# Loading q and k by head pairs in long runs: one window-attention and feed-forward kernel on one core

**Chip, cores, metric.** One Trainium2 chip, one core. The metric is the device time of one execution in microseconds (us). Runs of one set of comparisons share a chip; a run over 1.5% above the fastest of its kernel is slow, and comparisons use fast runs.

## The reference

```python
# q, k, v: (8 batches, 8 heads, 576 rows, 64), fp32; w_in 512x2048, w_out 2048x512
scores = q @ k.T / 8;  keep |i - j| <= 32;  attn = softmax(scores)
x = (attn @ v) as 4608 tokens x 512
h = x @ w_in;  g = h if h > 0 else exp(h) - 1
out = g @ w_out                                  # fp32
```

## The kernel before

The program is one loop of 144 steps. A step does the first layer of 256 hidden columns for 256 tokens (eight matmuls, an exponential on ScalarE, two VectorE operations) and, two steps later, the second layer (four matmuls). Attention is done in 36 pairs of 64-row blocks, placed between the steps. Four routes feed it, and these are what the change touches: q and k from DRAM, turned so that the head dimension lies on partitions; v, and a copy of it shifted by 64 partitions; and x, the attention's result, turned for the first layer.

```python
SJ = 6; SP_ = S // SJ                     # 96 partitions, 6 rows on each
def load_qk(b, which, part):              # part: whole batch or half
    z, nj = part
    ...
    nc.sync.dma_start(
        out=t[:, z * n:(z + 1) * n].rearrange("p (h x) -> p h x", h=H),
        in_=(q, k)[which][b, :, z * SP_ * nj:(z + 1) * SP_ * nj, :]
        .rearrange("h (p j) d -> p h (j d)", j=nj))

def rotate_v(b, m0=0, m1=VS - 1):         # the shifted copy of v
    e, o = V_e[b % 3], V_o[b % 3]
    nc.sync.dma_start(out=o[0:64, m0:m1], in_=e[64:128, m0:m1])
    nc.sync.dma_start(out=o[64:128, m0:m1], in_=e[0:64, m0 + 1:m1 + 1])

def transpose_rows(b, which):             # bf16 rows in DRAM -> qT or kT
    nc.sync.dma_start_transpose(
        out=keys_or_queries(b, which), in_=in_dram.pop((b, which)))

def x_dma(i):                             # pair i's x -> xT, also on SyncE
    x_st = st.pop(i)[3]
    nc.sync.dma_start_transpose(
        out=xT_of(i), in_=x_st.rearrange("p h d -> p (h d)"))

# ... (cut) the schedule: k0 is the step at which a batch's first pair begins
for b in range(2, B):
    k0 = begin[first_pair(b)]
    if b >= 3:
        kk = max(k0 - 26 if b < 5 else k0 - 36, 18)
        at(kk, "mid", load_qk, b, 0, WHOLE)
        at(kk + 1, "mid", load_qk, b, 1, WHOLE)
        for m in range(VS):
            at(kk + 2 + m // 3, "mid", load_v, b, m)
    if b < 5:   ...   # casts on POOL, transposes on TensorE
    else:       ...   # casts on ACT, rows to DRAM, transpose_rows
```

Batches 0 to 4 are turned by TensorE (casts for batches 2 to 4 on POOL, which is GpSimd), batches 5 to 7 by a DMA transpose of bf16 rows that were written back to DRAM. SyncE issues, in program order, the loads of q and k, the shifted copies, both kinds of DMA transpose and the outputs.

Names in the profile: PE is TensorE and PEld its weight loads, DVE is VectorE, ACT ScalarE, POOL GpSimd, SPq SyncE's queue. `f` is the tile in which q or k lands, `qkb` its bf16 cast, `Ve` is v and `Vo` its shifted copy, `in_dram` the rows written back, `x_st` and `xT` are x before and after its transpose. The granted clock is the share of TensorE's full clock that the chip allowed.

The softmax here doesn't subtract the row's maximum and nothing guards it: scores larger than these inputs give would overflow.

Of the kernel before, what the change touches and what calls it, by code (L numbers as in the profile page):

```python
# [9 lines left out]
FP32 = mybir.dt.float32  # L10
# [11 lines left out]
def kernel(  # L22
# [22 lines left out]
    SJ = 6  # L45
    SP_ = S // SJ
# [39 lines left out]
    def ps_tile(shape, dt, tag, name):  # L86
        return pools[tag].tile(shape, dt, tag=tag, name=name)
# [19 lines left out]
    def load_qk(b, which, part):  # L107
        z, nj = part
        if (b, which) not in qk_f:
            qk_f[b, which] = lpool.tile([SP_, H * SJ * D], FP32,  # L110
                                        tag=f"f{which}", name=f"f{which}")
        t = qk_f[b, which]
        n = H * nj * D
        nc.sync.dma_start(
            out=t[:, z * n:(z + 1) * n].rearrange("p (h x) -> p h x", h=H),
            in_=(q, k)[which][b, :, z * SP_ * nj:(z + 1) * SP_ * nj, :]
            .rearrange("h (p j) d -> p h (j d)", j=nj))
# [9 lines left out]
    def rotate_v(b, m0=0, m1=VS - 1):  # L127
        e, o = V_e[b % 3], V_o[b % 3]
        nc.sync.dma_start(out=o[0:64, m0:m1], in_=e[64:128, m0:m1])
        nc.sync.dma_start(out=o[64:128, m0:m1], in_=e[0:64, m0 + 1:m1 + 1])  # L130
# [41 lines left out]
    for m in (1, 2, 0, 3, 4):  # L172
        load_v(0, m)
    rotate_v(0, 0, 2)
    rotate_v(0, 2, VS - 1)
# [39 lines left out]
    def cast_qk(b, which, part, hps, eng):  # L215
        z, nj = part
        hp0, nh = hps[0], 2 * len(hps)
        n = H * nj * D
        s_ = qk_f[b, which][:, z * n + 2 * hp0 * nj * D:
                            z * n + (2 * hp0 + nh) * nj * D]  # L220
        s_ = _bap(s_, [s_.ap[0], [nj * D, nh], [D, nj], [1, D]])
        t = lpool.tile([SP_, nj, nh * D], BF16, tag=f"b{which}", name="qkb",
                       bufs=4)
        qk_b[b, which, z, hp0] = t
        copy_on(eng, _bap(t, [t.ap[0], [D, nh], [nh * D, nj], [1, D]]), s_)

    def keys_or_queries(b, which):
        if which == 0:
            return qT[b % 2]
        return kT[b % 2][:, KPAD:KPAD + HP * S].rearrange(  # L230
            "p (g s) -> p g s", g=HP)


    rows, in_dram = {}, {}

    def cast_rows(b, which, hp):
        if hp == 0:
            rows[b, which] = lpool.tile([SP_, SJ, H * D], BF16,
                                        tag=f"r{which}", name="rows", bufs=1)
        n = SJ * D  # L240
        s_ = qk_f[b, which][:, 2 * hp * n:(2 * hp + 2) * n]
        d_ = rows[b, which][:, :, 2 * hp * D:(2 * hp + 2) * D]
        nc.scalar.copy(  # L243
            _bap(d_, [d_.ap[0], [D, 2], [H * D, SJ], [1, D]]),
            _bap(s_, [s_.ap[0], [n, 2], [D, SJ], [1, D]]))

    def write_rows(b, which):
        t = dpool.tile([S, H * D], BF16, tag=f"d{which}", name="in_dram")
        in_dram[b, which] = t
        nc.scalar.dma_start(  # L250
            out=t.rearrange("(p j) c -> p j c", j=SJ), in_=rows.pop((b, which)))
# [5 lines left out]
    def transpose_qk(b, which, part, hps, evac, tag="t0"):  # L257
        z, nj = part
        src = qk_b.pop((b, which, z, hps[0]))
        nh = len(hps)  # L260
        W = 512 if nh > 1 else 1024
        pt = ps_tile([128, nh, W], BF16, tag, "ptx")
        for g in range(nh):
            for j in range(nj):
                nc.tensor.transpose(  # L265
                    pt[:, g, j * SP_:(j + 1) * SP_],
                    src[:, j, g * 128:(g + 1) * 128], ident[0:SP_, 0:SP_])
        n = SP_ * nj
        d = keys_or_queries(b, which)[:, hps[0]:hps[0] + nh, z * n:(z + 1) * n]
        pitch = d.ap[1][0] if nh > 1 else n  # L270
        copy_on(evac,
                _bap(d, [d.ap[0], [pitch, nh], [nj, SP_], [1, nj]]),
                _bap(pt, [pt.ap[0], [W, nh], [1, SP_], [SP_, nj]]))

# [70 lines left out]
    def x_evac(i):  # L345
        nc.vector.tensor_copy(xT_of(i), st.pop(i))  # L346
# [14 lines left out]
    def front_qk(part, tags):  # L361
        for g in range(2):
            hps = (2 * g, 2 * g + 1)
            cast_qk(0, 0, part, hps, nc.vector)
            cast_qk(0, 1, part, hps, nc.scalar)
            transpose_qk(0, 0, part, hps, nc.scalar, tags[g])
            transpose_qk(0, 1, part, hps, nc.vector, tags[2 + g])

    front_qk(HALF_A, ("h0", "h1", "y0", "y1"))
# [4 lines left out]
    front_qk(HALF_B, ("h0", "h1", "y0", "y1"))  # L374
    for fn in (pv, normalize, x_transpose, x_evac):
        for i in (0, 1):
            fn(i)
# [9 lines left out]
    rotate_v(1, 0, 2)  # L387
# [5 lines left out]
    rotate_v(1, 2, VS - 1)  # L393
# [25 lines left out]

    for i, tag in ((2, "s"), (3, "u")):  # L420
        at(0, "mid", scores, i, tag)
        at(1, "dve", mask, i)
        at(1, "mid", pv, i)
        at(2, "dve", normalize, i)
        at(2, "mid", x_transpose, i)
        at(3, "dve", x_evac, i)
    at(4, "dve", swap_pools)

    allh = tuple(range(HP))
    for part, kq in ((HALF_A, 8), (HALF_B, 16)):  # L430
        for which in range(2):
            at(kq - 1, "mid", cast_qk, 1, which, part, allh,
               (nc.scalar, nc.vector)[which])
            at(kq + which, "mid", transpose_qk, 1, which, part, allh,
               nc.scalar, "s")
    pair_at(4, 10)
    pair_at(5, 13)
# [5 lines left out]
    for i in range(8, NPAIR):  # L443
        kk = begin[i] = max(HALF * (i - 2) - 6, begin[i - 1] + 3)
        at(kk, "mid", scores, i)
        at(kk + 1, "dve", mask, i)
        at(kk + 1, "end", pv, i)
        at(kk + 2, "dve", normalize, i)
        at(kk + 2, "end", x_dma, i)
    for b in range(2, B):  # L450
        k0 = begin[first_pair(b)]
        if b >= 3:
            kk = max(k0 - 26 if b < 5 else k0 - 36, 18)
# [4 lines left out]
        if b < 5:  # L458
            for n in range(2 * HP):
                which, hp = n // HP, n % HP  # L460
                kk = k0 - (8 if b == 2 else 10) + n
                at(kk - 2 - b // 3, "mid", cast_qk, b, which, WHOLE, (hp,),
                   nc.gpsimd)
                at(kk, "mid", transpose_qk, b, which, WHOLE, (hp,), nc.scalar)
        else:
            for which in range(2):
                c0 = k0 - 27 + 8 * which
                for hp in range(HP):
                    at(c0 + (0, 1, 4, 5)[hp], "end", cast_rows, b, which, hp)
                at(c0 + 6, "mid", write_rows, b, which)  # L470
                at(c0 + 9, "mid", transpose_rows, b, which)
        at(k0 - HALF, "mid", rotate_v, b)
# [97 lines left out]
```

## Time and profile before

| | before |
|---|---|
| time, median (lowest to highest) | 337.28 us (336.18 to 338.95), 4 runs |
| profiled execution | span 340.9 us, granted clock 0.987 |
| first step, from the timeline | exponential at 28.2 us |
| last step | exponential at 333.2 us |

The prediction below shows the lines on which the reading of the kernel before rests: TensorE is busy nearly throughout, and the DMA engines for the first 150 us. Needed beside them are the landing times in the last part of its page (KB each, median us from issue to landing):

```profile
f<-in_q_dram SPq DMA_DIRECT2D x6, 1152.0 KB, 12.7
f<-in_k_dram SPq DMA_DIRECT2D x6, 1152.0 KB, 15.9
...
Ve<-in_v_dram POOLq DMA_DIRECT2D x24, 128.0 KB, 13.2
```

A whole q or k lands in 13 to 16 us.

### The profile page before, as it was taken

Reading aid. Unit: us, or ns where it says so; the run is one execution under the profiler, and the core shown is the slowest. Engines: PE = TensorE matmul, PEld = TensorE weight load, DVE = VectorE, ACT = ScalarE, POOL = GpSimd, SP = SyncE. Lnnn points to the kernel's source line nnn. Section 1 sums busy time; section 2 is a strip of 40 time slices with the busy share of each in tenths; the row PEclk is TensorE's granted clock in tenths of the full one; section 3 lists DMA queues with packets and bytes.
Section 4 is the critical chain, followed back from the end, with each engine's and each line's share of the span. In section 5 each row is a group of like instructions: output and inputs, shape, how many; then the busy total and the mean of one; then the engine's idle time right before and its main releaser. Section 6 shows DMA issues by size and latency. Waiting matters only on the chain.

```text
span 340.9 us, 7736 instructions
## 1 busy us (share of the span) xinstructions
PE 307.2 (90%) x3152; PEld 203.3 (60%) x3152; DVE 239.8 (70%) x446; ACT 171.8 (50%) x262; POOL 63.4 (19%) x84
## 2 busy tenths in 40 slices
PE   0358999789899999899999999799999999999994
PEld 0245666456566666566666666556666666666661
DVE  4445667577786779676877778377777787877663
ACT  1624264555556634587646666446645444434431
POOL 8352310094461129110011100000000000000000
PEclk9999999899999999999999999979999999999998
DMA  8999999999999999918999999969590420202011
GB/s 174 183 231 219 216 164 200 211 228 228 148 149 169 234 198 188 174 67 165 221 250 176 203 245 158 215 104 223 95 200 18 139 74 22 77 17 80 0 62 62
DMA packets 93862, 52.72 MB, mean 155 GB/s; under 512 B 67908, under 2 KB 87364, under 8 KB 93828
## 3 DMA queue, kind: packets, MB, share of 16 engines
q1 hardware_dynamic: 51428, 39.79, 55.8%
q0 software_dynamic: 41728, 8.92, 38.9%
q10 hardware_dynamic: 672, 3.54, 3.4%
q8 instruction: 24, 0.39, 0.5%
q14 instruction: 10, 0.08, 0.1%
HBM read 36.70 MB, written 12.98 MB: 146 GB/s over the span
## 4 chain that ended last, share of the span: by engine, by line
PE 74%; DMA 12%; DVE 8%; ACT 3%; issue 1%; SPq 0%; DVEq 0%
PE ps L489 34%; PE psY L516 31%; DMA xT<-x_st 8%; PE psS L312 3%; PE psS L284 3%; PE ptx L265 3%; DMA f<-in_k_dram 2%; DVE g_sb L502 2%; DVE m_sb L497 2%; ACT e_sb L495 2%; DMA Vo<-Ve 2%; DVE x_st L324 1%; ACT qkb L211 1%; DVE pm L300 1%; ACT pu L291 1%
## 5 line engine op out<-in xcount | busy, mean ns | idle before, releaser
L495 ACT ACTIVATE e_sb<-ps 128x512 f32<-128x512 f32 x144 | 86.0, 597 | 148.4 <-PE ps L489 146.4
L489 PE MATMUL ps<-xT,w_in_sb 128*128 128x256 bf16 x1152 | 153.1, 277 | 5.8 <-DVE xT L346 3.7
L516 PE MATMUL psY<-w_out_sb,g_sb 128*128 128x512 bf16 x576 | 149.7, 383 | 0.9 <-DVE g_sb L502 0.9
L489 PEld LDWEIGHTS <-w_in_sb 128*128 128x128 bf16 x1152 | 111.3, 99 | 44.6 <-issue 6.7
L502 DVE SCALAR_TENSOR_TENSOR g_sb<-ps,m_sb 128x512 bf16<-128x512 f32 x144 | 99.3, 690 | 13.8 <-DVE m_sb L497 0.5
L497 DVE TENSOR_SCALAR m_sb<-e_sb 128x512 bf16<-128x512 f32 x144 | 66.0, 459 | 60.2 <-ACT e_sb L495 58.7
L516 PEld LDWEIGHTS <-g_sb 128*128 128x128 bf16 x576 | 52.9, 98 | 39.8 <-DVE g_sb L502 1.5
L123 POOL DMA_DIRECT2D Ve<-in_v_dram x40 | 34.1, 858 | 94.5 <-PE psS L312 81.0
L291 ACT ACTIVATE pu<-psS 128x1024 bf16<-128x1024 f32 x36 | 36.5, 1019 | 3.2 <-PE psS L284 3.1
L265 PE MATMUL ptx<-ident,qkb 96*128 96x96 bf16 x240 | 17.7, 221 | 14.4 <-DVE qkb L213 12.0
L324 DVE TENSOR_TENSOR x_st<-psS,rc 128x512 bf16<-128x512 f32 x36 | 24.9, 691 | 6.4 <-DMA xT<-x_st 5.2
L300 DVE TENSOR_TENSOR pm<-pu,masks 128x1024 bf16<-128x1024 bf16 x36 | 26.4, 733 | 2.0 <-ACT pu L291 1.7
L213 POOL CAST qkb<-f 96x768 bf16<-96x768 f32 x24 | 20.8, 901 | 31.6 <-DMA f<-in_q_dram 22.0
L265 PEld LDWEIGHTS <-qkb 96*128 96x128 bf16 x240 | 14.5, 106 | 16.4 <-DVE qkb L213 12.5
L312 PEld LDWEIGHTS <-pm 128*64 128x64 bf16 x576 | 12.8, 115 | 17.0 <-DVE pm L300 11.4
L243 ACT CAST rows<-f 96x768 bf16<-96x768 f32 x24 | 19.7, 822 | 0.0
L284 PE MATMUL psS<-qT,kT 64*128 64x64 bf16 x576 | 15.3, 196 | 3.2 <-DVE x_st L324 1.8
L284 PEld LDWEIGHTS <-kT 64*128 64x128 bf16 x576 | 11.2, 98 | 10.7 <-issue 7.3
L312 PE MATMUL psS<-Vo,pm 128*64 128x65 bf16 x256 | 14.8, 203 | 2.6 <-DMA Vo<-Ve 1.8
L312 PE MATMUL psS<-Ve,pm 128*64 128x65 bf16 x320 | 16.8, 202 | 0.0
L211 ACT COPY qT<-ptx 128x576 bf16<-128x576 bf16 (+1 forms) x18 | 12.4, 689 | 4.1 <-PE ptx L265 4.1
L525 DVE COPY y_sb<-psY 128x512 f32<-128x512 f32 x18 | 12.3, 683 | 2.8 <-PE psY L516 2.8
(29 smaller groups left out, 64.3 us busy)
## 6 DMA issues: line engine op xcount, KB each, us to landing
out_dram<-y_sb SPq DMA_DIRECT2D x18, 512.0 KB, 3.4
f<-in_q_dram SPq DMA_DIRECT2D x6, 1152.0 KB, 12.7
f<-in_k_dram SPq DMA_DIRECT2D x6, 1152.0 KB, 15.9
in_dram<-rows ACTq DMA_DIRECT2D x6, 576.0 KB, 4.2
Vo<-Ve SPq DMA_DIRECT2D x12, 260.0 KB, 5.3
Ve<-in_v_dram POOLq DMA_DIRECT2D x24, 128.0 KB, 13.2
f<-in_q_dram SPq DMA_DIRECT2D x4, 576.0 KB, 9.7
f<-in_k_dram SPq DMA_DIRECT2D x4, 576.0 KB, 11.7
```

Of the source, the lines that this page charges most:

```text
L123: nc.gpsimd.dma_start(out=V_e[b % 3][p0:p1, m, :, 0:D], in_=v[b, :, lo + p0:lo + p1, :].rearrange("h p d -> p h d"))
L265: nc.tensor.transpose(pt[:, g, j * SP_:(j + 1) * SP_], src[:, j, g * 128:(g + 1) * 128], ident[0:SP_, 0:SP_])
L284: nc.tensor.matmul(psS[:, h % 2, hp * 128 + z * QB:hp * 128 + (z + 1) * QB], lhsT=kT[b % 2][base:base + 64, KPAD + hp * S + QB * qb - WIN: ...
L291: nc.scalar.activation(pu, _bap(psS, [psS.ap[0], [1, 1024]]), AX.Exp, scale=SCALE)
L300: nc.vector.tensor_mul(pm, pu, _bap(mm, [mm.ap[0], [0, H], [1, 2 * QB]]))
L312: nc.tensor.matmul(psS[QB * z:QB * (z + 1), par, hp * VD:(hp + 1) * VD], lhsT=pm[:, par * HP + hp, z * QB:(z + 1) * QB], rhs=vv[:, qb // 2 ...
L324: nc.vector.tensor_mul(x_st, _bap(psS, [psS.ap[0], [VD, HP], [512, 2], [1, D]]), _bap(rc, [rc.ap[0], [2, HP], [1, 2], [0, D]]))
L489: nc.tensor.matmul(ps[:, j, :], lhsT=w_in_sb[:, do, fo * 128:(fo + 1) * 128], rhs=xT[t][:, :, do, :], start=(do == 0), stop=(do == NDO - 1))
L495: nc.scalar.activation(e_sb, ps, AX.Exp)
L497: nc.vector.tensor_scalar(m_sb, e_sb, -1.0, None, ALU.add)
L502: nc.vector.scalar_tensor_tensor(g_sb, psH.pop(kk), 0.0, m_t.pop(kk), ALU.max, ALU.min)
L516: nc.tensor.matmul(psY[t][ts], lhsT=g_sb[:, j, ts * 128:(ts + 1) * 128], rhs=w_out_sb[:, s * FG + j, :], start=(s == 0 and j == 0), stop=( ...
```

## The change

The intent: longer runs in DRAM (4608 bytes in place of 1536) on all 128 partitions; all transposes with full tiles (128 rows in place of 96); five batches, not three, turned by DMA; no POOL casts; and the shifted v made by VectorE, which takes twelve DMAs of 260 KB off the queues. The core of the diff:

```diff
-    SJ = 6
-    SP_ = S // SJ
+    NC = 128 // HP            # 32 partitions for each of 4 head pairs
+    SJ = S // NC              # 18 rows on each
 def load_qk(b, which, part):
-        nc.sync.dma_start(
-            out=t[:, z * n:(z + 1) * n].rearrange("p (h x) -> p h x", h=H),
-            in_=(q, k)[which][b, :, z * SP_ * nj:(z + 1) * SP_ * nj, :]
-            .rearrange("h (p j) d -> p h (j d)", j=nj))
+        src = (q, k)[which][b, :, z * NC * nj:(z + 1) * NC * nj, :].rearrange(
+            "(g h) (c j) d -> g c h (j d)", h=2, j=nj)
+        for h in range(2):
+            nc.sync.dma_start(out=t[:, h, :], in_=src[:, :, h, :])
 def rotate_v(b, m0=0, m1=VS - 1):
-        nc.sync.dma_start(out=o[0:64, m0:m1], in_=e[64:128, m0:m1])
-        nc.sync.dma_start(out=o[64:128, m0:m1], in_=e[0:64, m0 + 1:m1 + 1])
+        nc.vector.tensor_copy(o[0:64, m0:m1], e[64:128, m0:m1])
+        nc.vector.tensor_copy(o[64:128, m0:m1], e[0:64, m0 + 1:m1 + 1])
 # ... (cut) casts in three groups of 768 columns on ACT; order of the front
-            kk = max(k0 - 26 if b < 5 else k0 - 36, 18)
+            kk = max(k0 - 30, 18)
-        if b < 5:             # POOL casts, TensorE transposes
+        if b == 2:            # ACT casts, TensorE transposes
-        else:                 # b = 5, 6, 7 through DRAM rows
+        else:                 # b = 3 to 7 through DRAM rows
```

More of the change, by code (lines that the diff above doesn't have):

```diff
@@ L108, in load_qk @@
         z, nj = part
-        if (b, which) not in qk_f:
-            qk_f[b, which] = lpool.tile([SP_, H * SJ * D], FP32,
-                                        tag=f"f{which}", name=f"f{which}")
-        t = qk_f[b, which]
-        n = H * nj * D
-        nc.sync.dma_start(
-            out=t[:, z * n:(z + 1) * n].rearrange("p (h x) -> p h x", h=H),
-            in_=(q, k)[which][b, :, z * SP_ * nj:(z + 1) * SP_ * nj, :]
-            .rearrange("h (p j) d -> p h (j d)", j=nj))
+        t = lpool.tile([128, 2, nj * D], FP32, tag=f"f{which}{nj}",
+                       name=f"f{which}")
+        qk_f[b, which, z] = t
+        src = (q, k)[which][b, :, z * NC * nj:(z + 1) * NC * nj, :].rearrange(
+            "(g h) (c j) d -> g c h (j d)", h=2, j=nj)
+        for h in range(2):
+            nc.sync.dma_start(out=t[:, h, :], in_=src[:, :, h, :])
     def load_v(b, m):
@@ L171 @@
             load_qk(0, which, part)
-    for m in (1, 2, 0, 3, 4):
+    for m in (1, 0, 2, 3, 4):
         load_v(0, m)
-    rotate_v(0, 0, 2)
-    rotate_v(0, 2, VS - 1)
     load_w_in(0)
@@ L213, in copy_on, with cast_qk @@
             eng.tensor_copy(d_, s_)
-    def cast_qk(b, which, part, hps, eng):
+    def cast_qk(b, which, part, j0, n, eng):
         z, nj = part
-        hp0, nh = hps[0], 2 * len(hps)
-        n = H * nj * D
-        s_ = qk_f[b, which][:, z * n + 2 * hp0 * nj * D:
-                            z * n + (2 * hp0 + nh) * nj * D]
-        s_ = _bap(s_, [s_.ap[0], [nj * D, nh], [D, nj], [1, D]])
-        t = lpool.tile([SP_, nj, nh * D], BF16, tag=f"b{which}", name="qkb",
-                       bufs=4)
-        qk_b[b, which, z, hp0] = t
-        copy_on(eng, _bap(t, [t.ap[0], [D, nh], [nh * D, nj], [1, D]]), s_)
+        if (b, which, z) not in qk_b:
+            qk_b[b, which, z] = lpool.tile(
+                [128, nj, 2 * D], BF16, tag=f"b{which}{nj}", name="qkb")
+        t = qk_b[b, which, z]
+        copy_on(eng,
+                t[:, j0:j0 + n, :].rearrange("p j (h d) -> p h j d", h=2),
+                qk_f[b, which, z][:, :, j0 * D:(j0 + n) * D].rearrange(
+                    "p h (j d) -> p h j d", d=D))
     def keys_or_queries(b, which):
         if which == 0:
-            return qT[b % 2]
-        return kT[b % 2][:, KPAD:KPAD + HP * S].rearrange(
-            "p (g s) -> p g s", g=HP)
-    rows, in_dram = {}, {}
-    def cast_rows(b, which, hp):
-        if hp == 0:
-            rows[b, which] = lpool.tile([SP_, SJ, H * D], BF16,
-                                        tag=f"r{which}", name="rows", bufs=1)
-        n = SJ * D
-        s_ = qk_f[b, which][:, 2 * hp * n:(2 * hp + 2) * n]
-        d_ = rows[b, which][:, :, 2 * hp * D:(2 * hp + 2) * D]
-        nc.scalar.copy(
-            _bap(d_, [d_.ap[0], [D, 2], [H * D, SJ], [1, D]]),
-            _bap(s_, [s_.ap[0], [n, 2], [D, SJ], [1, D]]))
+            return qT[b % 2].rearrange("p g s -> p (g s)")
+        return kT[b % 2][:, KPAD:KPAD + HP * S]
+    in_dram = {}
     def write_rows(b, which):
-        t = dpool.tile([S, H * D], BF16, tag=f"d{which}", name="in_dram")
+        t = dpool.tile([HP * S, 2 * D], BF16, tag=f"d{which}", name="in_dram")
         in_dram[b, which] = t
         nc.scalar.dma_start(
-            out=t.rearrange("(p j) c -> p j c", j=SJ), in_=rows.pop((b, which)))
+            out=t.rearrange("(p j) c -> p j c", j=SJ),
+            in_=qk_b.pop((b, which, 0)))
     def transpose_rows(b, which):
@@ L255, in transpose_rows, with transpose_qk @@
             out=keys_or_queries(b, which), in_=in_dram.pop((b, which)))
-    def transpose_qk(b, which, part, hps, evac, tag="t0"):
+    def transpose_qk(b, which, part, j0, n, evac, tag="t0"):
         z, nj = part
-        src = qk_b.pop((b, which, z, hps[0]))
-        nh = len(hps)
-        W = 512 if nh > 1 else 1024
-        pt = ps_tile([128, nh, W], BF16, tag, "ptx")
-        for g in range(nh):
-            for j in range(nj):
-                nc.tensor.transpose(
-                    pt[:, g, j * SP_:(j + 1) * SP_],
-                    src[:, j, g * 128:(g + 1) * 128], ident[0:SP_, 0:SP_])
-        n = SP_ * nj
-        d = keys_or_queries(b, which)[:, hps[0]:hps[0] + nh, z * n:(z + 1) * n]
-        pitch = d.ap[1][0] if nh > 1 else n
+        src = qk_b[b, which, z]
+        pt = ps_tile([128, 1024 if n <= 8 else 2048], BF16, tag, "ptx")
+        for j in range(n):
+            nc.tensor.transpose(
+                pt[:, j * 128:(j + 1) * 128], src[:, j0 + j, :], ident)
+        d = keys_or_queries(b, which)
         copy_on(evac,
-                _bap(d, [d.ap[0], [pitch, nh], [nj, SP_], [1, nj]]),
-                _bap(pt, [pt.ap[0], [W, nh], [1, SP_], [SP_, nj]]))
+                _bap(d, [d.ap[0], [S, HP], [nj, NC], [1, n]],
+                     z * NC * nj + j0),
+                _bap(pt, [pt.ap[0], [NC, HP], [1, NC], [128, n]]))
     st = {}
@@ L343, in xT_of, with x_evac @@
         return xT[t][:, z, :, :]
-    def x_evac(i):
-        nc.vector.tensor_copy(xT_of(i), st.pop(i))
+    def x_evac(i, eng=nc.vector):
+        copy_on(eng, xT_of(i), st.pop(i))
     def x_dma(i):
@@ L359, with front_cast, front_transpose @@
     nc.scalar.activation(warm, warm, AX.Exp)
-    def front_qk(part, tags):
-        for g in range(2):
-            hps = (2 * g, 2 * g + 1)
-            cast_qk(0, 0, part, hps, nc.vector)
-            cast_qk(0, 1, part, hps, nc.scalar)
-            transpose_qk(0, 0, part, hps, nc.scalar, tags[g])
-            transpose_qk(0, 1, part, hps, nc.vector, tags[2 + g])
-    front_qk(HALF_A, ("h0", "h1", "y0", "y1"))
+    SPLIT = ((0, 5), (5, 4))
+    def front_cast(which, part, eng):
+        for j0, n in SPLIT:
+            cast_qk(0, which, part, j0, n, eng)
+    def front_transpose(which, part, evac, tags):
+        for (j0, n), tag in zip(SPLIT, tags):
+            transpose_qk(0, which, part, j0, n, evac, tag)
+    for (j0, n), th, ty in zip(SPLIT, ("h0", "h1"), ("y0", "y1")):
+        cast_qk(0, 0, HALF_A, j0, n, nc.vector)
+        cast_qk(0, 1, HALF_A, j0, n, nc.scalar)
+        transpose_qk(0, 0, HALF_A, j0, n, nc.scalar, th)
+        transpose_qk(0, 1, HALF_A, j0, n, nc.vector, ty)
     for i, tag in ((0, "s"), (1, "u")):
@@ L373 @@
         mask(i)
-    front_qk(HALF_B, ("h0", "h1", "y0", "y1"))
-    for fn in (pv, normalize, x_transpose, x_evac):
-        for i in (0, 1):
-            fn(i)
+    rotate_v(0, 0, 2)
+    front_cast(0, HALF_B, nc.vector)
+    front_cast(1, HALF_B, nc.scalar)
+    for i in (0, 1):
+        pv(i)
+    for i in (0, 1):
+        normalize(i)
+    front_transpose(0, HALF_B, nc.scalar, ("h0", "h1"))
+    x_transpose(0)
+    x_evac(0, nc.scalar)
+    front_transpose(1, HALF_B, nc.vector, ("y0", "y1"))
+    x_transpose(1)
+    x_evac(1, nc.scalar)
     gate(w_out_sb[0:1, NFO // 4 - 1, D_MODEL - 1:D_MODEL])
@@ L386 @@
         load_w_out(c)
-    rotate_v(1, 0, 2)
     gate(w_in_at(3))
@@ L392 @@
         load_v(1, m)
-    rotate_v(1, 2, VS - 1)
     for which in range(2):
@@ L417, in pair_at @@
         at(kk + 3, "dve", x_evac, i)
+    at(2, "dve", rotate_v, 0, 2, VS - 1)
     for i, tag in ((2, "s"), (3, "u")):
@@ L422 @@
         at(1, "dve", mask, i)
-        at(1, "mid", pv, i)
-        at(2, "dve", normalize, i)
-        at(2, "mid", x_transpose, i)
-        at(3, "dve", x_evac, i)
+        at(2, "mid", pv, i)
+        at(3, "dve", normalize, i)
+        at(3, "mid", x_transpose, i)
+        at(4, "dve", x_evac, i)
     at(4, "dve", swap_pools)
-    allh = tuple(range(HP))
     for part, kq in ((HALF_A, 8), (HALF_B, 16)):
         for which in range(2):
-            at(kq - 1, "mid", cast_qk, 1, which, part, allh,
+            at(kq - 1, "mid", cast_qk, 1, which, part, 0, SJ // 2,
                (nc.scalar, nc.vector)[which])
-            at(kq + which, "mid", transpose_qk, 1, which, part, allh,
+            at(kq + which, "mid", transpose_qk, 1, which, part, 0, SJ // 2,
                nc.scalar, "s")
-    pair_at(4, 10)
-    pair_at(5, 13)
+    at(10, "dve", rotate_v, 1, 0, 2)
+    at(17, "dve", rotate_v, 1, 2, VS - 1)
+    pair_at(4, 9)
+    pair_at(5, 12)
     pair_at(6, 18)
@@ L449 @@
         at(kk + 2, "end", x_dma, i)
+    starts = set(begin.values()) | {9, 12, 18}
+    LEAD = 18
     for b in range(2, B):
@@ L457 @@
                 at(kk + 2 + m // 3, "mid", load_v, b, m)
-        if b < 5:
-            for n in range(2 * HP):
-                which, hp = n // HP, n % HP
-                kk = k0 - (8 if b == 2 else 10) + n
-                at(kk - 2 - b // 3, "mid", cast_qk, b, which, WHOLE, (hp,),
-                   nc.gpsimd)
-                at(kk, "mid", transpose_qk, b, which, WHOLE, (hp,), nc.scalar)
-        else:
-            for which in range(2):
-                c0 = k0 - 27 + 8 * which
-                for hp in range(HP):
-                    at(c0 + (0, 1, 4, 5)[hp], "end", cast_rows, b, which, hp)
-                at(c0 + 6, "mid", write_rows, b, which)
-                at(c0 + 9, "mid", transpose_rows, b, which)
-        at(k0 - HALF, "mid", rotate_v, b)
+        groups = [(which, j0) for which in range(2) for j0 in (0, 6, 12)]
+        if b == 2:
+            free = [f for f in range(17, k0) if f not in starts]
+            for n, (which, j0) in enumerate(groups):
+                at(free[max(n - 1, 0)], "end", cast_qk, b, which, WHOLE, j0,
+                   6, nc.scalar)
+                at(free[n + 1], "mid", transpose_qk, b, which, WHOLE, j0,
+                   6, nc.scalar)
+        else:
+            free = [f for f in range(k0 - LEAD, k0) if f not in starts]
+            for n, (which, j0) in enumerate(groups):
+                at(free[n], "end", cast_qk, b, which, WHOLE, j0, 6, nc.scalar)
+                if j0 == 12:
+                    at(free[n], "end", write_rows, b, which)
+                    at(free[n] + 4, "mid", transpose_rows, b, which)
+        at(k0 - HALF - 1, "dve", rotate_v, b)
     order = [(z, n) for z in range(2) for n in range(HALF)]
```

## The prediction

Four engines for the new loads are my premise, which the trace of the kernel before does not show. The 1.5 us charged for completion is my estimate too; in that trace the seven loads of k with no other load of q or k behind them landed 0.5 to 1.1 us after their last packet.

> **What bounds the kernel now.** I read the busy table, the slices, a table of windows, the chain of waits and the DMA view, in that order. The busy table and the slices of the page:
>
> ```profile
> PE 307.2 (90%) x3152; PEld 203.3 (60%) x3152; DVE 239.8 (70%) x446; ACT 171.8 (50%) x262; POOL 63.4 (19%) x84
> ...
> PE   0358999789899999899999999799999999999994
> ...
> DMA  8999999999999999918999999969590420202011
> ```
>
> TensorE is full except in the first three slices and a few dents (slices 8, 10, 25). The DMA engines are full too, for the first 150 us: loads have little room to get slower. The window from 226 to 334 us:
>
> ```profile
> 226.00:334.00 108.00, 108.00 (x1013) 71.00 (x1012) 81.05 (x152) 50.53 (x80) 0.00 (x0) 1.00 0.34 80
> ```
>
> The first number after the length is TensorE's busy time: no gap. In the chain of waits (start, length, what) the same eight matmuls show a start, a cold one and a warm one:
>
> ```profile
> 17.01 5.62 DMA Vo<-Ve
> ...
> 26.32 1.87 PE ps L489 x8
> ...
> 37.59 0.87 PE ps L489 x8
> ```
>
> A step (8 matmuls of the first layer, 4 of the second) costs 0.87 + 0.86 = 1.73 us; 144 steps make 249 us. The rest is attention and transposes on TensorE (some 45 us), 26.3 us before the first step, a few stalls and the last store. So the bound is TensorE, if its operands come in time. In time means, from the timeline (start of each step's exponential): step 7 at 43.7, 15 at 61.6, 17 at 69.5, 20 at 77.9, 22 at 83.1, 26 at 94.2, 32 at 107.5, 44 at 134.1, 56 at 161.0, 80 at 208.3, 96 at 244.1.
>
> The DMA view between 2 and 7 us, where only q and k move:
>
> ```profile
> GB/s 123 74 61 55 74 104 197 264 264 264 326 326 362 362 326 289 258 209 246 258 264 258 258 197 190 184 197 233 252 233 215 227 178 246 233 264 215 209 221 252
> ...
> q1 hardware_dynamic: 1478, 1.12, 102.3%
> ```
>
> All 16 engines are busy (102%) and move 224 GB/s on the mean, 362 at best: one engine has shown 362 / 16 = 22.6 GB/s.
>
> [...] Before, a q load has 96 rows slowest on both sides: 16, and the view above agrees (a peak of 362 GB/s needs many engines). After, the DRAM side is (4 head pairs, 32 rows, a run) against 128 partitions[...]. No load of the kernel before has such a shape, so its trace cannot confirm it. I looked at the built instruction: the counts 4 and 32 stand in it unmerged. [...] m_sb takes 427 ns at the median and 1042 at most, the long ones while POOL casts. [...]
>
> **The change part by part.**
> What helps. The shifted v: the 5.62 us of DMA on the chain becomes two VectorE copies of 1040 columns, which by the 560 ns of a 768-column cast (fp32) I estimate at 0.5 to 1 us each: some -4 us at the front. TensorE transposes in the loop fall from 192 (96 rows, 0.42 us per 6 at full clock) to 72 (128 rows, estimate 0.055 us each, from 0.39 us per 4 with overlap): 192 / 6 x 0.42 = 13.4, less 72 x 0.055 = 4.0, so up to -9 us; as they overlap with their neighbours, nearer -4. ACT's 24 casts of rows (822 ns) become 36 (estimate the same, 768 columns each), 19.7 to 29.6 us, while its PSUM copies for batches 2 to 4 fall from 24 x 0.635 = 15.2 to 6 x 0.8 = 4.9: even. POOL's 24 casts go, with what they cost VectorE (m_sb 66.0 - 144 x 0.427 = 4.5 us, pm about 2 more); the full-size shift copies (2080 columns, estimate 0.7 to 1.2 us, two per batch) take about that back. Pairs 4 and 5 start one step earlier, which should end the waits of TensorE for xT near step 16 (some 2 us). By itself all this is worth some -10 to -15 us.
>
> What hurts. q and k are 18.9 MB. On 4 engines of 22.6 GB/s they move at 90 GB/s, 13 us for q or k of a batch, 26 us for both, 209 us for all eight, where before both landed in about 16 us beside other traffic. [...] From 8 to 17 us before, queues overlap on one engine (DMA share 2.19 in the windows' table) while q and k still lost half their rate to v. So I charge v at 5 us a batch (half of its 9.3 us), a weight chunk at 2 to 3 us, 1.5 us for completion. [...] Walking through it:
>
> - Batch 0: 2.4 + 26 + 4.5 (v) + 5 (two weight chunks) + 1.5 = k's second half at 39.5 us. TensorE's order now puts both second-half transposes before x is finished, so the first step waits for that half too: plus cast, transpose and copies, 3.5 us: 43 us (26.3 before).
> - Batch 1, first half: 38 + 13 + 9 + 1.5 = 61.5; step 7 wants it at 43 + 17.4 = 60.4: step 7 at 62. Second half, gated on the weights: 85.5; step 15 wants it at 80: 86.
> - Batch 2: q at 101.5, step 17 wants it at 90: 102. k at 114.5, step 20 wants it at 110: 115. The casts sit in ACT's program order in front of the next exponential, so each lateness stops the loop.
> - Batch 3, loads queued behind: q 130.5 for step 22 (120): 131. k 143.5 for step 26 (140): 144.
> - Batch 4: issued at step 28, 148 us; 26 + 5 + 3 (rows, transposes): 182. Pair 9's x transpose stands behind it and step 32 wants it at 156: 184.
> - Batch 5: issued at step 44, 208; 38 us with outputs and transposes: 246, in front of pair 15's x for step 56 (232): 246.
> - Batch 6: issued at step 64, 262; 300 for step 80 (294): 300. Batch 7: issued at step 80; 338 for step 96 (332): 338.
> - The remaining 340.9 - 244.1 = 97 us run at TensorE's pace: 435. Some seven stops[...] restart at the low clock, about 2 us each (two steps at 1.87 for 0.87): 449, say **450 us**.
>
> **The rivals.**
> Rival A, the loads use all 16 engines (the instruction is reshaped on the way[...]). For it: the schedule looks tuned, and runs of 2304 and 4608 bytes in place of 768 and 1536 should only help. [...] Then only the helpful part remains: about 323 us.
> Rival B, 16 engines, and VectorE or ACT becomes the bound: VectorE is busy 6.4 of each 7.9 us (four steps)[...]; casts on ACT stand before exponentials. TensorE's lag of two steps hides about 2 us of it: 330 to 338 us.
> Rival C, 4 engines, but a worse rate per engine, such as the 224 / 16 = 14 GB/s mean: q and k alone take 337 us: 550 us or more. Against it: 362 GB/s shows that the mean comes from sharing, not from one engine.
> Rival D, 4 engines, but hidden by prefetch: the loads for batches 4 to 7 are issued 30 steps before their use, some 60 us, and take 37. Against it: the x transposes behind them are wanted after 3 to 12 steps. If TensorE could run on, 400 us or a little under.
>
> **Range and chances.** Four engines: 0.9 (two independent signs, none measured here). Within that, 385 to 530 us holds most: the lower end from D and a fast engine, the upper from C in part. Sixteen engines, 0.1: mostly faster (A), some within 2% (B). So 450 us, 385 to 530; faster 0.09, same 0.02, slower 0.89.
>
> **What would show it.** The DMA view: f loads landing later than 12 us per half and 20 us or more per whole, and in stretches with loads alone a rate near 90 GB/s with the DMA share near 0.25 where it was 1.0. The waits: large entries of ACT or VectorE casts on "DMA f<-in_q_dram" and "in_k_dram", and of TensorE on "DMA xT<-x_st". The first step near 43 us; steps 22, 32 and 96 near 131, 184 and 338 us. POOL without casts; m_sb close to 427 ns; 108 transposes. I am wrong if loads run at over 200 GB/s, or if the first step starts before 26 us; the size is wrong if steps 32 to 96 take under 120 us (154 here, 137 before).

## The result, and the profile after

| | before | after |
|---|---|---|
| median (lowest to highest), 4 runs each | 337.28 us (336.18 to 338.95) | 477.56 us (472.78 to 479.78) |
| ratio | 1 | 1.413 (1.400 to 1.427) |
| profiled execution | 340.9 us, clock 0.987 | 474.4 us, clock 0.877 |

Ratios here are the mean time of one kernel's fast runs over that of the other's of the same rounds, so they are not quite the ratio of the medians quoted. The kernel became 41% slower.

From the page of the kernel after: busy times, then slices of the span (tenths; PEclk is the granted TensorE clock).

```profile
PE 321.9 (68%) x3020; PEld 205.8 (43%) x3020; DVE 245.4 (52%) x464; ACT 172.1 (36%) x258; POOL 42.8 (9%) x60
...
PE   0145838767419500699970699618996799999995
...
PEclk9999979977958855699986699876999799999999
DMA  9959969645429969357995999945997773202111
```

TensorE has holes up to slice 31, and a lowered clock after most of them: 0.50 from 64.7 to 71.3 us and from 163.7 to 197.6 us, 1.00 from 200 to 245 us. The eight first-layer matmuls at 193.49 us, after a stop of 32.8 us, took 1.89 us; those at 37.59 us in the kernel before took 0.87. DMA does not look busier than before: it is below the digit of before in 14 of the 40 slices and above it in 8. In the twelve slices with TensorE at five tenths or less, DMA is at 2 to 6 tenths in eight and at 9 in four. The chain that ended last, by engine and by line, on the same page:

```profile
PE 38%; DMA 33%; issue 17%; SPq 5%; DVE 3%; POOL 2%; ACT 1%; DVEq 0%; POOLq 0%; ACTq 0%
```

Before, DMA was 12% of that chain. The waits (us in total, times, longest):

```profile
PE ps L488 <- DMA xT<-x_st: 53.4, 3, 32.8
...
DVE x_st L303 <- DMA xT<-x_st: 30.7, 4, 15.2
ACT qkb L207 <- DMA f<-in_k_dram: 29.3, 3, 16.2
...
ACT qkb L207 <- DMA f<-in_q_dram: 19.1, 2, 12.2
PEld L263 <- DMA kT<-in_dram: 18.8, 2, 11.9
```

Casts wait for q and k, TensorE waits for x behind them, and it waits for turned keys. The DMA view of the kernel after between 130 and 140 us, where it moves only q and k (the hardware queue, q1) and v (the software queue, q0):

```profile
DMA  2223223223322332233223322332233223322332
...
DMA packets 412, 0.95 MB, mean 95 GB/s; under 512 B 212, under 2 KB 212, under 8 KB 412
...
q1 hardware_dynamic: 206, 0.92, 23.9%
q0 software_dynamic: 206, 0.03, 3.9%
```

This is the signature: 0.92 MB of q and k in 10 us is 92 GB/s, on 24% of the 16 engines' time, which is close to four engines fully busy (0.239 x 16 = 3.8). The trace's packet records, counted by how many are under way at once, say the same more directly: over the whole execution the 4608-byte packets of q and k are most often four at a time (71% of the time in which any is under way), and 16 at a time in e2 below. Also to be seen: 206 packets of one queue to 206 of the other. A long packet of q or k (4608 bytes) and a short one of v (128 bytes) take turns.

### The profile page after: what moved, and what is told of

Its sections match the earlier page's. It is cut to its first block, busy times and chain, and to the rows that moved or that the text cites. A ratio compares the mean times of both kernels' runs of the same rounds, so it can differ in the third digit from the quotient of the medians.

```text
span 474.4 us, 7465 instructions
## 1 busy us (share of the span) xinstructions
PE 321.9 (68%) x3020; PEld 205.8 (43%) x3020; DVE 245.4 (52%) x464; ACT 172.1 (36%) x258; POOL 42.8 (9%) x60
## 3 DMA queue, kind: packets, MB, share of 16 engines
q0 software_dynamic: 41728, 8.92, 27.9%
## 4 chain that ended last, share of the span: by engine, by line
PE 38%; DMA 33%; issue 17%; SPq 5%; DVE 3%; POOL 2%; ACT 1%; DVEq 0%; POOLq 0%; ACTq 0%
PE ps L488 17%; PE psY L515 17%; DMA Ve<-in_v_dram 10%; DMA w_in_sb<-in_moe_w_in_dram 6%; DMA f<-in_q_dram 6%; DMA kT<-in_dram 4%; DMA f<-in_k_dram 4%; DMA xT<-x_st 2%; SPq L238 2%; POOL Ve L121 2%; SPq L525 2%; PE psS L291 1%; PE psS L263 1%; SPq L115 1%; DVE m_sb L496 1%
## 5 line engine op out<-in xcount | busy, mean ns | idle before, releaser
L488 PE MATMUL ps<-xT,w_in_sb 128*128 128x256 bf16 x1152 | 160.9, 286 | 80.9 <-DMA xT<-x_st 53.4
L488 PEld LDWEIGHTS <-w_in_sb 128*128 128x128 bf16 x1152 | 114.6, 102 | 125.1 <-issue 39.1
L515 PE MATMUL psY<-w_out_sb,g_sb 128*128 128x512 bf16 x576 | 158.2, 399 | 1.3 <-DVE g_sb L501 0.9
L496 DVE TENSOR_SCALAR m_sb<-e_sb 128x512 bf16<-128x512 f32 x144 | 62.6, 435 | 118.4 <-ACT e_sb L494 116.5
L515 PEld LDWEIGHTS <-g_sb 128*128 128x128 bf16 x576 | 55.3, 102 | 45.5 <-issue 7.8
L207 ACT CAST qkb<-f 128x768 bf16<-128x768 f32 (+3 forms) x42 | 34.6, 830 | 48.4 <-DMA f<-in_k_dram 29.3
L303 DVE TENSOR_TENSOR x_st<-psS,rc 128x512 bf16<-128x512 f32 x36 | 24.9, 692 | 31.8 <-DMA xT<-x_st 30.7
L246 PE MATMUL ptx<-ident,qkb 128*128 128x128 bf16 x108 | 12.2, 277 | 30.4 <-DVE qkb L209 15.7
L263 PEld LDWEIGHTS <-kT 64*128 64x128 bf16 x576 | 11.6, 100 | 31.4 <-DMA kT<-in_dram 18.8
L246 PEld LDWEIGHTS <-qkb 128*128 128x128 bf16 x108 | 9.7, 126 | 32.5 <-DVE qkb L209 15.9
L209 DVE CAST qkb<-f 128x640 bf16<-128x640 f32 (+2 forms) x6 | 3.6, 619 | 22.7 <-DMA f<-in_k_dram 14.7
L523 ACT COPY y_sb<-psY 128x512 f32<-128x512 f32 x18 | 10.5, 584 | 2.0 <-PE psY L515 2.0
## 6 DMA issues: line engine op xcount, KB each, us to landing
Ve<-in_v_dram POOLq DMA_DIRECT2D x24, 128.0 KB, 27.9
```

The costliest lines, as they stand in the source:

```text
L207: nc.scalar.copy(d_, s_)
L263: nc.tensor.matmul(psS[:, h % 2, hp * 128 + z * QB:hp * 128 + (z + 1) * QB], lhsT=kT[b % 2][base:base + 64, KPAD + hp * S + QB * qb - WIN: ...
L303: nc.vector.tensor_mul(x_st, _bap(psS, [psS.ap[0], [VD, HP], [512, 2], [1, D]]), _bap(rc, [rc.ap[0], [2, HP], [1, 2], [0, D]]))
L488: nc.tensor.matmul(ps[:, j, :], lhsT=w_in_sb[:, do, fo * 128:(fo + 1) * 128], rhs=xT[t][:, :, do, :], start=(do == 0), stop=(do == NDO - 1))
L496: nc.vector.tensor_scalar(m_sb, e_sb, -1.0, None, ALU.add)
L515: nc.tensor.matmul(psY[t][ts], lhsT=g_sb[:, j, ts * 128:(ts + 1) * 128], rhs=w_out_sb[:, s * FG + j, :], start=(s == 0 and j == 0), stop=( ...
```

## The experiments

### Is it the number of engines?

**e2_rows_first**: the kernel after with partition 4 x (row block) + (head pair) in place of 32 x (head pair) + (row block). DRAM's slowest count becomes 32 in place of 4, with 128 on the other side. The run length stays.

```diff
-            "(g h) (c j) d -> g c h (j d)", h=2, j=nj)     # then t[:, h, :]
+            "(g h) (c j) d -> c g h (j d)", h=2, j=nj)
 # rows written to DRAM, and the copies out of PSUM, put the order right again
-            out=t.rearrange("(p j) c -> p j c", j=SJ),
+            out=t.rearrange("(g c j) x -> c g (j x)", g=HP, j=SJ),
```

> The kernel after, with partition p = 4 x row block + head pair in place of 32 x head pair + row block: the DRAM side of each load then has the 32 row blocks slowest, 128 on the other side, so 16 engines, with the same two DMAs per load, the same bytes and the same run lengths. The copy out of PSUM and the write to DRAM rows follow the new order. Theory: as e1, 315 to 335 us; e1 and e2 within 3% of each other, since only the engine count matters. Rivals: as for e1, 400 us or more.

Measured: 345.38 us (341.34 to 346.83, 4 runs), ratio to before 1.017 (1.006 to 1.027), correct. The DMA view of this kernel between 72 and 76 us, with loads alone:

```profile
DMA packets 395, 1.60 MB, mean 400 GB/s; under 512 B 48, under 2 KB 48, under 8 KB 395
...
q1 hardware_dynamic: 395, 1.60, 100.2%
```

The same packets, the same bytes, 400 GB/s in place of 92 (92 was measured beside v, so v's share is missing in it). Undoing only the order of the dimensions takes back 132 of the 140 us. It misses the expected 315 to 335 us by 10, and e1 below is 3.7% away where at most 3% was expected; nor does it reach the 323 us that the prediction's Rival A promised for 16 engines. That is taken up below. (The profiled execution of e2 was a slow one, 346.83 us; what is read from it here are rates and waits, not its time.)

**e1_by_pair**: the kernel after with four loads per tile, one for each head pair, 32 partitions each, so that all 16 engines work.

```diff
-        for h in range(2):
-            nc.sync.dma_start(out=t[:, h, :], in_=src[:, :, h, :])
+        for g in range(HP):
+            nc.sync.dma_start(out=t[g * NC:(g + 1) * NC], in_=src[g])
```

> The kernel after, with one thing altered: each load of q or k is four DMAs, one per head pair, of 32 partitions by 2 heads, in place of two DMAs by head whose DRAM side has the 4 head pairs slowest. 32 rows are slowest on both sides now, so 16 engines. Theory (the loads ran on 4 engines, all else of the change is mildly good): 315 to 335 us[...]; loads landing in under 15 us. Rival 1 (the schedule, casts on ACT in front of the exponentials or the x transposes behind loads stop the loop whatever the loads' rate): 400 us or more. Rival 2 (long runs are slow by themselves on this DRAM layout): above 400 us too, with the DMA share near 1 and a rate under 150 GB/s.

Measured: 358.14 us (357.73 to 363.56, 5 runs), ratio 1.058 (1.048 to 1.068): the expectation missed. All 16 engines worked, but the DMA view from 66 to 72 us shows them at half rate:

```profile
DMA packets 657, 1.26 MB, mean 211 GB/s; under 512 B 395, under 2 KB 395, under 8 KB 655
...
q1 hardware_dynamic: 328, 1.20, 96.7%
q0 software_dynamic: 327, 0.04, 10.6%
```

97% busy for 200 GB/s of q and k. In the packet records 15 or 16 of the 4608-byte packets are under way at once here, but each takes 356 ns at the median, against 178 ns in the view of e2 above. Why a packet takes twice as long is not shown. So two things go with the rate of e2: a slowest count of 32 on both sides and not 4, and partitions spread over the whole width in one DMA. The second rests on e1 alone, which also has twice as many DMAs as e2; that rival was not tested on this kernel (in e4b below eight times as many DMAs cost 10 us).

**e3_two_engines**: the dose. Each load is cut into halves of two head pairs, whose slowest count is 2.

```diff
+            for g in (0, 2):
+                nc.sync.dma_start(out=t[g * NC:(g + 2) * NC, h, :],
+                                  in_=src[g:g + 2, :, h, :])
```

> The kernel after, with each load in four DMAs like e1, but two head pairs of one head each: 2 is slowest on the DRAM side, so 2 engines. Dose: theory says q and k move at half of after's rate (46 GB/s in place of 92), 51 us per batch, so some 25 us more for each of 7 batches behind the first and 26 for the first: 620 to 720 us. If the number of DMAs or the length of runs mattered and not the engine count, it would be like e1.

Measured: 653.6 us (one run). Its DMA view from 130 to 140 us:

```profile
q1 hardware_dynamic: 167, 0.40, 11.6%
```

That is 0.40 MB of q and k on 11.6% of the engines' time, 40 GB/s on two engines (two load packets at a time for 77% of the loading). It lies in the expected range. The time follows the count: 16, 4 and 2 engines give 345, 478 and 654 us.

**e4a_heads_four** and **e4b_heads_all**: the other direction, in the kernel *before*. Each load is cut into eight, one per head. In e4a a row's partition is permuted so that the slowest DRAM count is 4; in e4b it stays 96. The number of DMAs and the bytes are the same.

```diff
+        for h in range(H):
+            s_ = src[h]                                       # e4a and e4b
+            s_ = _bap(s_, [[w, 4], [4 * w, 24], [1, w]])      # e4a only
+            nc.sync.dma_start(out=t[:, z * n + h * w:z * n + (h + 1) * w], in_=s_)
```

> The kernel before, with its q and k loads issued head by head (8 DMAs each) with the DRAM rows in an order that leaves 4 slowest; the results are wrong on purpose (rows permuted), the bytes and run lengths of 768 and 1536 are those of before. Theory (the engine count alone makes the loss, no other part of the change is needed): 420 to 500 us. Rival (the loss needs the change's deeper use of DMA: rows for five batches, half the loads issued behind others): under 380 us.

> Control for e4a_heads_four: the kernel before with the same eight loads per q or k half, one per head, but with the 96 rows as the slowest dimension on both sides (16 engines), so that the number of DMAs is the same and only the engines differ. If four engines are what cost e4a its 133 us: 338 to 355 us, and loads alone at over 200 GB/s. If it was the eight-fold number of DMAs (issue time on SyncE): over 420 us.

Measured: e4a 471.76 us, e4b 347.98 us (one run each). e4a's rows are permuted, so it computes something else; the comparison with the reference lets it pass all the same, as with inputs of 0.1 times normal draws the scores presumably hardly differ from 0 (this was not measured). Eight times as many DMAs cost 10 us; the four engines cost 124 us more, in a kernel that has nothing else of the change. Both lie in their expected ranges. The 1536-byte load packets are most often four at a time in e4a and 16 in e4b. So the engine count is necessary (e2) and sufficient (e4a) for the slowdown. Over the loads from SyncE's queue, slowest counts of 2, 4 and 32 or 96 had most often 2, 4 and 16 packets under way, at 40, 92 and 400 or 224 GB/s (the last with the kernel before's short runs); e1, with 32 in blocks of 32 partitions, had 15 or 16 at 200 GB/s.

### Where did the surplus over the prediction come from?

The result is 27.6 us above the predicted 450. I first took v for the term that was too small, since in the kernel after a v block lands in 27.9 us (13.2 before) and shares its turns with q and k.

**e7_no_later_v**: the kernel after without the v loads of batches 3 to 7 (wrong result).

```diff
-            for m in range(VS):
-                at(kk + 2 + m // 3, "mid", load_v, b, m)
```

> The changed kernel without the v loads of batches 3 to 7 (their shifted copies stay and take stale v: wrong result on purpose). In the changed kernel v's 128-byte packets stand packet for packet between those of q and k on the four loaded engines. Theory: this is the term that my sum had too small (v at 5 us a batch); without these loads steps 32 to 96 fall from 182 us to 140 to 160, the total to 440 to 460. Rival: the surplus is order on SyncE's queue (x behind loads and row transposes), not v: steps 32 to 96 stay at 170 to 185 us, total 465 to 480.

Measured: 449.42 us (one run), 28 us less; steps 32 to 96 took 169.4 us in place of 181.9. The total lies in the theory's range; the stretch lies between the two, 0.6 us short of the rival's. So neither expectation held as a whole. Over five batches v is worth 28 / 5 = 5.6 us each, which is what the prediction charged (5 us). v is a real cost, but not the one that was too small: in that stretch the stops at turned keys stay (10.9 us in place of 11.9).

**e8_loads_on_pool**: the kernel after with the loads of batches 3 to 7 on POOL's queue, so that nothing on SyncE's queue stands behind them.

```diff
-            nc.sync.dma_start(out=t[:, h, :], in_=src[:, :, h, :])
+            eng = nc.gpsimd if b >= 3 else nc.sync
+            eng.dma_start(out=t[:, h, :], in_=src[:, :, h, :])
```

> The changed kernel, four engines per load as before, with the q and k loads of batches 3 to 7 issued on POOL's queue, in front of their batch's v, so that no x transpose, row transpose or output on SyncE's queue stands behind them. Theory (order): what costs after step 28 is the place of x behind 26 us of loads in one in-order queue; the bytes themselves (26 + 5 to 10 us a batch on four engines against 32 to 35 us of TensorE work a batch) nearly fit. Steps 32 to 96 then take 137 to 150 us and the total is 390 to 420. Rival (bandwidth): x, row transposes and outputs also need the four loaded engines and wait there packet for packet, whichever queue they come from; steps 32 to 96 stay over 165 us and the total over 450.

Measured: 478.07 us (475.7 to 480.43, 2 runs), steps 32 to 96 in 182.9 us. My theory (order in the queue) fell; the rival's numbers hold. But the run is less clean than its edit: q and k did not stay on four engines. In the packet records most often eight of their 4608-byte packets on POOL's queue are under way at once, where the kernel after has four, and each takes 348 ns (median) in place of 191. So it shows that taking the loads off SyncE's queue did not help, and not what would happen with only their order changed. SyncE's issues in this kernel's timeline (start, length; first from 158 us, then from 224 us), of row transposes, with no load of q or k before or behind them on that queue:

```profile
160.02 15.44 SPq L239 DMA_TRANSPOSE qT<-in_dram  x1
...
178.63 17.23 SPq L239 DMA_TRANSPOSE kT<-in_dram  x1
```

```profile
226.38 15.69 SPq L239 DMA_TRANSPOSE qT<-in_dram  x1
...
252.31 17.77 SPq L239 DMA_TRANSPOSE kT<-in_dram  x1
```

In e8 the six row transposes issued while q and k were loading took 15.4 to 21.0 us, the four issued after the last load 2.1 to 3.4. In the fastest version (e9 below) all ten take from 2.0 to 8.1 us. Here SyncE cannot even finish issuing one, and x behind it waits, although the loads come from another queue. That the queues share the DMA engines fits these times, but it is my reading: no packet record here names its engine.

**e10_short_packets**: do the queues really take turns by packets? The kernel after with the landing tile of whole loads padded after every six rows, so that a packet is 1536 bytes and not 4608; four engines and the bytes stay.

```diff
-        t = lpool.tile([128, 2, nj * D], ...)
+        t = lpool.tile([128, 2, 3, 6 * D + 16], ...)          # whole loads only
-            nc.sync.dma_start(out=t[:, h, :], in_=src[:, :, h, :])
+            nc.sync.dma_start(out=t[:, h, :, 0:6 * D], in_=src[:, :, h, :])
```

> The changed kernel with the landing tile of whole q and k loads (batches 2 to 7) padded after every six rows, so that a packet is 1536 bytes and not 4608; still four engines, same bytes. The kernel before moved 1536-byte packets in 65 ns at best (23.6 GB/s), 4608-byte packets take 180 (25.6): loads alone should keep 85 to 92 GB/s. Theory (one packet for one): where v and loads share the four engines, v gets about three packets in the time of one before, so v lands in 8 to 15 us in place of 28 (median), and the total falls towards that of the run without later v (449): 445 to 465. Rival (engines share by time or bytes, or v is slow for another reason): v's landing stays over 22 us, total 472 to 482.

Measured: 483.32 us (482.33 to 484.31, 2 runs). The DMA views of this kernel from 175 to 180 us (q and k beside v) and from 145 to 150 us (q and k alone):

```profile
DMA packets 482, 0.39 MB, mean 78 GB/s; under 512 B 249, under 2 KB 482, under 8 KB 482
...
q1 hardware_dynamic: 248, 0.36, 52.1%
```

```profile
DMA packets 329, 0.50 MB, mean 100 GB/s; under 512 B 2, under 2 KB 329, under 8 KB 329
```

Beside v, 233 load packets (482 - 249) stand against some 230 of v in 5 us, where the kernel after had 103 to 103 (half of its 206 in 10 us). One packet for one holds, and v lands in 17.4 us (median) in place of 27.9, which is between the 8 to 15 of the theory and the 22 of the rival. The total does not fall as expected, and it is just above the rival's range too: loads slow from 100 to 72 GB/s while v runs. v's turns are only taken sooner; what the four engines have to move is the same. So e10, and e7 with 28 us less when v is gone, fit a loop that is bounded by the sum of work on these engines and not by its division. That its order does not matter is not shown: e8, the test of it, moved the loads to other engines too.

### What would the rest of the change be worth?

**e6_before_dve_shift**: the kernel before with only the shifted v made by VectorE (v's first blocks, the shifted copies and pairs 2 and 3 are placed as in the change).

```diff
-        nc.sync.dma_start(out=o[0:64, m0:m1], in_=e[64:128, m0:m1])
-        nc.sync.dma_start(out=o[64:128, m0:m1], in_=e[0:64, m0 + 1:m1 + 1])
+        nc.vector.tensor_copy(o[0:64, m0:m1], e[64:128, m0:m1])
+        nc.vector.tensor_copy(o[64:128, m0:m1], e[0:64, m0 + 1:m1 + 1])
```

> The kernel before with one part of the change alone: the shifted v made by VectorE copies and not by DMA. Theory: the 5.62 us of that DMA on the chain before the first step goes, and q, k and v have the queue to themselves: first step 3 to 5 us earlier, total 332 to 336 us. Rival: the front is bound by the loads of q, k and v themselves (the DMA engines stay full), so the first step moves by under 1.5 us, and the copies cost VectorE what they save: 336 to 341 us.

Measured: 340.35 us (338.5 to 342.46, 6 runs), ratio 1.009 (1.003 to 1.015). The rival was right. Its chain of waits:

```profile
16.96 0.43 DVE Vo L129
...
17.42 0.68 DVE Vo L130
...
18.13 0.57 DVE qkb L211
...
25.99 1.86 PE ps L489 x8
```

The copies take 1.1 us where the DMA took 5.62, and yet the first step starts at 25.99 us, 0.33 earlier: after them VectorE still casts the second half (at 18.13), as it did beside the DMA. The DMA stood on the chain only because it ended a little later.

**e5_rows_first_later**: e2 with two numbers moved. In e2, TensorE's largest stop was 11.2 us at step 32, for pair 9's x; SyncE's issues in its timeline:

```profile
92.40 1.29 SPq L115 DMA_DIRECT2D f<-in_q_dram  x2
94.46 5.17 SPq L238 DMA_TRANSPOSE qT<-in_dram  x1
99.68 1.25 SPq L115 DMA_DIRECT2D f<-in_k_dram  x2
100.97 5.44 SPq L329 DMA_TRANSPOSE xT<-x_st  x2
```

A row transpose holds the queue for 5.2 us, then two loads go first, then x.

```diff
-            kk = max(k0 - 30, 18)
+            kk = max(k0 - 24, 18)
-                    at(free[n] + 4, "mid", transpose_rows, b, which)
+                    at(free[n] + 5, "mid", transpose_rows, b, which)
```

> e2_rows_first (the change with partitions ordered so that all 16 engines load) with two numbers of the schedule moved: loads of batches 3 to 7 six steps later (24 steps before their batch's first pair in place of 30), the transposes of rows one step later, so that pair 9's x transpose stands in front of batch 4's loads and of batch 3's row transpose on SyncE's queue. Theory: e2 lost 11.4 us at step 32 and 3.0 us at pair 15 to that order, and nothing else of size: 345.4 - 14 = 331 us, 327 to 335, that is 2% under the kernel before. Rival: the stop is the x transpose itself, or moves to the next pair or to late keys of batches 4 to 7 (which now have only 6 steps, 12 us, to land before their first cast): 340 to 350 us.

Measured: 332.77 us (331.05 to 334.26, 6 runs), ratio 0.987 (0.983 to 0.992), correct; expected 331. The stop at step 32 is gone.

**e9_tuned**: e5 with three moves into idle time that its timeline showed.

```diff
-            kk = max(k0 - 24, 18)
+            kk = max(k0 - (22 if b == 4 else 24), 18)
-    at(2, "dve", rotate_v, 0, 2, VS - 1)
+    at(0, "dve", rotate_v, 0, 2, VS - 1)
     # and, in the front, rotate_v(0, 0, 2) ahead of the two masks
```

> e5_rows_first_later with three small moves: the first shifted copies of v stand before the masks on VectorE (which sat idle 1.8 us there), batch 0's other shifted copies before step 0 in place of step 2 (VectorE sat idle 2.4 us there, and TensorE waited 2.5 us for them at 27.7), and batch 4's loads two steps later, behind pair 11's x transpose (TensorE waited 2.4 us for that at 118.3). Theory: each wait goes as it stood in the trace: 1 + 2 + 2.4 = some 5 us: 326 to 330 us, 2.5 to 3.5% under the kernel before. Rival: the waits move to the next thing (v landing, loads late for their first cast): 331 to 335 us.

Measured: 325.69 us (324.71 to 326.16, 6 runs), ratio 0.962 (0.958 to 0.967), correct: faster than both kernels. From its page:

```profile
PE 297.0 (92%) x3020; PEld 196.0 (61%) x3020; DVE 244.2 (76%) x464; ACT 171.7 (53%) x258; POOL 42.8 (13%) x60
...
PE   0387989898999999999999999999999999999993
```

## Why the prediction was right, and where its sizes were off

The direction and the mechanism were right: four engines for q and k, 90 GB/s predicted and 92 measured. The time was 450 us (range 385 to 530), the result 477.56. Point by point:

| step (start of its exponential, us) | before | predicted | after |
|---|---|---|---|
| 0 | 28.2 | 43 | 42.9 |
| 7 | 43.7 | 62 | 59.6 |
| 15 | 61.6 | 86 | 88.2 |
| 17 | 69.5 | 102 | 98.7 |
| 20 | 77.9 | 115 | 114.6 |
| 22 | 83.1 | 131 | 123.2 |
| 26 | 94.2 | 144 | 149.5 |
| 32 | 107.5 | 184 | 195.4 |
| 56 | 161.0 | 246 | 267.2 |
| 80 | 208.3 | 300 | 336.6 |
| 96 | 244.1 | 338 | 377.3 |

The first row compares unlike things: the 43 was meant for the first step's matmuls (26.3 before), and these began at 41.0.

- **Walking the loads step by step** was right to a few us up to step 26, 8 us at most off. From step 32 to 96 it was too short: 154 predicted, 182 measured. At step 96 the walk was 39 us early; that the total is only 27.6 us off is in part because the 14 us charged after step 96 for restarts did not fall there (the last stretch took 97 us, as predicted without them).
- **Low clock.** The prediction charged 14 us at the end for restarts. The same 3020 recorded matmuls took 321.9 us in the kernel after and 297.0 in e9 (clocks 0.877 and 0.997): 24.9 us, so 11 too little if the clock is the whole difference. A part of it lies in the stretches of the table.
- **The 38 us a batch "with outputs and transposes"** was the mis-sized term: 26 for q and k, 5 for v, so 7 for the rest. The stretches in question took 45.0 us (steps 44 to 56, batch 5), 52.5 us (64 to 80, batch 6) and 40.7 us (80 to 96, batch 7): 24 of the 28 us. By difference the 7 us became 14, 21 and 10, restarts at a low clock included. Row transposes are the part of it that can be seen. In the kernel after SyncE's timeline has:

```profile
347.21 16.09 SPq L238 DMA_TRANSPOSE qT<-in_dram  x1
363.39 1.22 SPq L329 DMA_TRANSPOSE xT<-x_st  x1
```

  SyncE is held for 16 us, and x goes after it. TensorE stopped for 11.9 us at 309.8 us, for turned keys of batch 5 (their transpose held SyncE for 18.4 us), and for 6.9 us at 363.8 us, when this transpose had kept VectorE from reusing x's buffers. Together 19 us of stops that the walk did not have. With the 11 us of clock that is 30 us against the 27.6 missing; the terms overlap (some stops predicted earlier came out shorter), so this is a fit in size, not an exact account. No run took the row transposes away, so their share is not shown by experiment.
- **x behind the loads of its queue** fits the kernel after: of the 256-byte packets of the transposes issued behind k's load at 176 us some 300 start between 178 and 183 us, and the other 2900 only from 190 us, when k's packets end. But the wait does not need it: in e8, where no load but only a row transpose stands in front of x on its queue, TensorE's longest wait for x was 37.8 us.
- **v at 5 us a batch** fits: 5.6 us by e7 (one run).
- **Small slips in the sums** that change nothing: 6 x 0.8 is 4.8, batch 0's terms add up to 39.4, and of the long `m_sb` two of twelve have no POOL cast beside them.
- **Rival A (16 engines, 323 us)** was wrong about the schedule: with 16 engines and nothing else the time is 345 us (e2), because x still stood behind a row transpose and two loads. With that order mended it is 333, and 326 after tuning. So the helpful parts, together with the schedule moves of e5 and e9, are worth 12 to 14 us, as its sum of "-10 to -15" said; whether such moves would help the kernel before was not tested, so a part of the agreement may be luck. Its one part that was tested alone, "-4 us at the front" for the shifted v, is not there (e6). How the gain divides among transposes, casts and POOL was not tested.
- **Rival B** (VectorE or ACT as the bound): VectorE's two shifted copies of 1040 columns took 0.43 and 0.68 us in e6, the full-size ones 0.70 at the median, and m_sb 435 ns on the mean in the kernel after (459 before); no sign of it.
- **Rival C** (14 GB/s per engine): refuted by 92 / 4 = 23 GB/s.
- **Rival D** (hidden by prefetch): refuted by the result, and e8, where no x stands behind the loads in their queue, took the same time.

## What to carry to other kernels

Before rewriting a load for longer runs, look at the slowest count of each new access pattern (4 in place of 96 cost e4a 124 us against e4b), and look in the trace for the pair "all queued, yet the DMA share is a quarter" (24% here): few engines fully busy look like an idle DMA system. Put a large count outermost on both sides (32 and 96 had 16 packets under way here, 4 and 2 had 4 and 2), and keep all 128 partitions in one transfer (e1 is the one run behind this last). When loads are mended, look next at what is issued behind them on the same queue: the last 6% here came from letting a small, urgent transpose go before large, early loads.
